# Attention steps and chunks of the gated projection moved in a written task list, values stored without zero blocks, and slopes that read PSUM

## The chip, the core and the metric

The kernel runs on one core of a Trainium2 chip. The metric is device time in microseconds (us), the median of three executions. A separate, profiled execution gives the trace that everything below is read from. The names of the engines are those of the profile: PE is the matrix engine, PEld its weight loads, DVE the vector engine, ACT the scalar engine, POOL the general engine and SP the engine that issues the DMAs.

## The reference

Three stages follow each other, all in float32:

```python
# 1. attention, q, k, v: (4 batches, 8 heads, 576, 64)
scores = q @ k.T / 8, masked: heads 0-3 see the last 32 positions,
         heads 4-7 every fourth of the last 128
x = softmax(scores) @ v                     # -> (2304, 512)
# 2. gated projection, d_ff = 1536
x = (sigmoid(x @ w_gate) * (x @ w_val)) @ w_out
# 3. second projection, d_ff = 2048
h = x @ w_in
g = maximum(h, 0) + alpha * minimum(h, 0)
out = g @ w_out2
```

## The kernel before

Every large product is made of three float16 matmuls ("passes": high by high, high by low, low by high half). So each weight and each activation is scaled and split into a high half (ACT) and a low half (DVE or POOL).

Attention is done per batch `b` in two half-batches, `hb = 2b` (plain window) and `hb = 2b + 1` (dilated). Its steps are `qk_mm` and `qk_sub` (scores and maximum), `exponent`, `p_sums`, `p_scale`, `transpose`, `p_hi`, `p_lo`, the splits of the values `v_hi` and `v_lo`, the products `pv_mm`, and `pv_x`, which splits the result into `xh[b]`. In `pv_mm` two heads of a pair share one matmul: 64 rows hold the keys of two heads, and the stationary value tile is 64 x 128, with one head's values in columns 0 to 63 and the other's in 64 to 127; the block of the wrong head is zero. To write these zeros, `v_hi` and `v_lo` run twice with the scale times 0 or 1 per row (`sides`, `v_scale`). A half-batch has 19 blocks x 3 passes x 2 pairs = 114 such matmuls; seven of the eight half-batches use them (the first uses float32, `pv32_mm`).

The gated projection of a batch has 12 chunks `m`: `gv_mm` for "g" and "v" (24 matmuls of 288 columns each), `gv_sigmoid` on ACT, `gv_multiply` on DVE, and `gv_halves`, the split into `gt[b, m]`. Then come four output columns `d` (`o1_mm`, 72 matmuls each, and `o1_y`, which stores the result). Three pairs of PSUM banks rotate among all g, v and o products.

What stands where is written out by hand. The head of the program, with attention of batches 0 and 1, all of batch 0's projection and the preparation of its weights, is the task list `FIRST`: a row such as `g 1 0 0` is a call, and each engine runs its instructions in the order of the calls. After it a loop goes over batches 1 to 3. In it, `attention(b + 1)` gives two tables, `before` and `after`, of steps keyed by chunk (0 to 11) or column (12 to 15), and `prepare` takes steps from a queue `steps` that decode, sum, split and store the weights of the second projection. Each call adds to a budget, and a step is taken when the budget covers its cost. The last batch ("late") also begins the second projection: `y_high`, `y_low` and `unit_short` between the columns of `o1_mm`.

The second projection is computed by a seven-product scheme on quarters. After the loop, 16 calls of `unit(j, k)` (four blocks `j` of tokens, four `k` each) make the hidden values; between their seven products, `spare()` puts the products of the output (`out2_mm`) of the block before. In a unit, `c1`, `c2` and `c4` are copied from PSUM by ACT (`copy`), `plus` adds such a copy to another product on DVE, `relu` makes the negative part on ACT, and `slopes` (two DVE instructions of 256 columns) adds it with its slope. The sums of quarters run on POOL (`g_sums`), and `high` and `g_low` split the hidden values.

## Time and profile before

| | us |
|---|---|
| median of 3 executions (886.60 to 889.74) | 888.07 |
| the profiled execution | 886.76 |
| its span, first to last instruction | 885.0 |
| PE busy | 831.8 (94%) |
| DVE busy | 660.7 (75%) |
| ACT busy | 450.8 (51%) |
| POOL busy | 300.4 (34%) |

A busy share is an average over stages with different limits: 94% of PE is made of long stretches in which it never waits, and of a few in which it does. What a change is worth is decided in the second kind. A row of the timeline gives, in brackets, how long the engine had been idle before it and what ended that. A granted clock of 1.00 is 2.4 GHz, one of 0.50 is 1.2 GHz; a figure between is a mean over the stretch.

### The profile page before, as it was taken

Reading aid. Unit: us, or ns where it says so; the run is one execution under the profiler, and the core shown is the slowest. Engines: PE = TensorE matmul, PEld = TensorE weight load, DVE = VectorE, ACT = ScalarE, POOL = GpSimd, SP = SyncE. Lnnn points to the kernel's source line nnn. Section 1 sums busy time; section 2 is a strip of 40 time slices with the busy share of each in tenths; the row PEclk is TensorE's granted clock in tenths of the full one; section 3 lists DMA queues with packets and bytes.
Section 4 is the critical chain, followed back from the end, with each engine's and each line's share of the span. In section 5 each row is a group of like instructions: output and inputs, shape, how many; then the busy total and the mean of one; then the engine's idle time right before and its main releaser. Section 6 shows DMA issues by size and latency. Waiting matters only on the chain.

```text
span 885.0 us, 19452 instructions
## 1 busy us (share of the span) xinstructions
PE 831.8 (94%) x8196; PEld 684.9 (77%) x8196; DVE 660.7 (75%) x1039; ACT 450.8 (51%) x739; POOL 300.4 (34%) x264
## 2 busy tenths in 40 slices
PE   7789687999999999999999989997999999999998
PEld 5467465777777777777788768886888888888887
...
GB/s 330 288 171 156 192 119 154 54 76 157 81 38 199 206 82 156 25 29 320 240 148 237 331 252 224 340 222 193 264 185 190 273 281 192 202 302 203 128 217 81
DMA packets 85175, 166.81 MB, mean 188 GB/s; under 512 B 5344, under 2 KB 57696, under 8 KB 85088
## 3 DMA queue, kind: packets, MB, share of 16 engines
...
HBM read 137.24 MB, written 28.31 MB: 187 GB/s over the span
## 4 chain that ended last, share of the span: by engine, by line
PE 52%; DVE 23%; ACT 10%; DMA 5%; issue 5%; POOL 3%; SPq 1%; ACTq 0%; DVEq 0%; POOLq 0%
PE banks L1206 14%; PE banks L963 13%; PE banks L589 12%; PE banks L631 10%; DVE plain L187 3%; DVE plain L183 3%; DVE temp_w L1009 2%; ACT junk L194 2%; DVE plain L179 2%; DMA plain_dram<-plain 2%; DVE gf L607 2%; DVE halves L823 2%; DVE temp_y L1009 2%; PE banks L323 1%; DMA w_dram<-halves 1%
## 5 line engine op out<-in xcount | busy, mean ns | idle before, releaser
L589 PE MATMUL banks<-xh,w_gv 128*128 128x288 f16 x2304 | 295.0, 289 | 7.5 <-DVE sc L156 3.3
L589 PEld LDWEIGHTS <-w_gv 128*128 128x128 f16 x2304 | 224.2, 99 | 67.9 <-issue 6.6
L963 PE MATMUL banks<-yh,w_i 128*128 128x256 f16 x1536 | 190.0, 275 | 13.1 <-ACT temp_y L1018 6.5
L963 PEld LDWEIGHTS <-w_i 128*128 128x128 f16 x1536 | 151.3, 99 | 33.6 <-issue 13.5
L631 PE MATMUL banks<-gt,w_o 128*128 128x288 f16 x1152 | 146.5, 288 | 3.6 <-DVE gf L607 1.8
L631 PEld LDWEIGHTS <-w_o 128*128 128x128 f16 x1152 | 112.2, 98 | 33.0 <-issue 3.0
L1206 PEld LDWEIGHTS <-g_gv 128*128 128x128 f16 x780 | 76.6, 98 | 9.1
L1206 PE MATMUL banks<-w,g_gv 128*128 128x256 f16 x612 | 75.5, 273 | 0.0
L1058 POOL TENSOR_TENSOR yh<-temp_y 128x512 f32<-128x512 f32 x16 | 27.0, 1690 | 131.6 <-DVE temp_y L1009 126.9
L164 POOL TENSOR_SCALAR sc<-sc 128x1 f32<-128x1 f32 x35 | 11.6, 333 | 167.8 <-DVE sc L160 167.7
L1009 DVE SCALAR_TENSOR_TENSOR temp_w<-neg,sc,temp_w 128x256 f32<-128x256 f32 x48 | 55.5, 1194 | 10.9 <-ACT neg L1001 10.8
L168 POOL TENSOR_TENSOR gt<-gf,gt 128x576 f16<-128x576 f32 x24 | 38.3, 1595 | 73.7 <-ACT gt L614 73.6
L1206 PEld LDWEIGHTS <-g_g 128*128 128x128 f16 x564 | 55.2, 98 | 6.4
L187 DVE SCALAR_TENSOR_TENSOR plain<-words,plain 128x512 uint32<-128x512 uint32 x68 | 56.9, 858 | 1.2
L194 ACT ACTIVATE junk<-plain 128x1024 bf16<-128x1024 f32 (+1 forms) x36 | 36.3, 1009 | 39.4 <-DVE plain L198 21.7
L602 ACT ACTIVATE sg<-banks,sc 128x576 f32<-128x576 f32 x48 | 35.3, 735 | 39.5 <-PE banks L589 28.5
L607 DVE SCALAR_TENSOR_TENSOR gf<-banks,sg 128x576 f32<-128x576 f32 x48 | 35.9, 749 | 25.1 <-PE banks L589 24.2
L183 DVE SCALAR_TENSOR_TENSOR plain<-words,plain 128x512 uint32<-128x512 uint32 x68 | 49.3, 746 | 1.2
L614 ACT ACTIVATE gt<-gf 128x576 f16<-128x576 f32 x48 | 32.4, 674 | 34.9 <-DVE gf L607 34.9
L1206 PE MATMUL banks<-w,g_g 128*128 128x256 f16 x396 | 48.3, 273 | 0.0
L179 DVE TENSOR_SCALAR plain<-words 128x512 uint32<-128x512 uint32 x68 | 34.6, 530 | 14.0 <-DMA plain_dram<-plain 6.2
L388 POOL TENSOR_TENSOR s<-s,rs 128x1152 f32<-128x1152 f32 (+1 forms) x9 | 17.3, 1925 | 72.0 <-DVE rs L383 65.5
...
## 6 DMA issues: line engine op xcount, KB each, us to landing
...
```

What stands on the lines that cost most here:

```text
L168: engine.tensor_tensor(out=lo, in0=src, in1=hi, op=ALU.subtract)
L179: nc.vector.tensor_scalar(out=d, in0=hi, scalar1=3, scalar2=0x3FFFFFFF, op0=ALU.logical_shift_left, op1=ALU.bitwise_and)
L183: nc.vector.scalar_tensor_tensor(out=d, in0=hi, scalar=0xC0000000, in1=d, op0=ALU.bitwise_and, op1=ALU.bitwise_or)
L187: nc.vector.scalar_tensor_tensor(out=d, in0=lo, scalar=29, in1=d, op0=ALU.logical_shift_right, op1=ALU.bitwise_or)
L194: nc.scalar.activation(junk[:, :src.shape[1]], src, AF.Square, accum_out=dst)
L589: nc.tensor.matmul(ps[:, h, :], lhsT=a, rhs=x_[:, H2 * h:H2 * h + H2], start=(kk == 0 and i == 0), stop=(kk == KD - 1 and i == 2),)
L602: nc.scalar.activation(halves(sg), ps, AF.Sigmoid, scale=sgx[b][:, m:m + 1])
L607: nc.vector.scalar_tensor_tensor(out=halves(gf), in0=ps, scalar=2.0 ** -15, in1=halves(sg), op0=ALU.mult, op1=ALU.mult)
L631: nc.tensor.matmul(ps[:, h, :], lhsT=a, rhs=x_[:, H2 * h:H2 * h + H2], start=(m == 0 and z == 0), stop=(m == M1 - 1 and z == 2),)
L963: nc.tensor.matmul(o, lhsT=h, rhs=l, start=(new and v == 0 and q == 1), stop=(q == total_), skip_group_check=True,)
L1009: nc.vector.scalar_tensor_tensor(out=temps[x_][:, c], in0=t[:, c], scalar=slope[:, u + v:u + v + 1], in1=src[:, c], op0=ALU.mult, op1=ALU.add,
L1206: nc.tensor.matmul(ps[:, H4 * t:H4 * t + H4].rearrange("p (c f) -> p c f", c=2), lhsT=a, rhs=x_, start=(first and k == 0 and t == 0 and z ...
```

## The change

It has four parts.

1. Values without zero blocks: `vh` holds the values once. `v_hi` and `v_lo` are one instruction each, and `v_scale` is gone. `pv_mm` takes 32 rows (one head) and a 64-column stationary tile, with the head choosing the upper or lower half of the output partitions: twice as many matmuls of the same width.
2. Slopes read PSUM: `plus` writes its sum back to PSUM (onto the bank of product 2, and onto that of product 7 for the last quarter), and `relu` and `slopes` read it there.
3. `FIRST` is written in another order, and takes in chunks 1 and 2 of batch 1 (before it held chunk 0 alone: three chunks now), the steps 0 to 6 of the attention of batch 2 (`hb` 4), and three calls of `prepare`. The loop for batch 1 starts at chunk 3 and skips those steps. Two `gt` tiles of batch 1 get places of their own.
4. In the loop, the `after` steps of a column come inside its loop over `m` (for `d == 2` at `m == 6`).

```diff
+    EARLY = 3
+    DONE = 7
-    NQ, NK, NV = 2 * NB * 64, 2 * (S + WINDOW), NB * P
+    NQ, NK, NV = 2 * NB * 64, 2 * (S + WINDOW), NB * 64
+    def v_hi(hb):
+        nc.scalar.activation(v_half(hb, 0), vc[hb], AF.Copy, scale=s_x[:, hb // 2:hb // 2 + 1])
+
+    def v_lo(hb):
+        nc.vector.scalar_tensor_tensor(
+            out=v_half(hb, 1), in0=vc[hb], scalar=s_x[:, hb // 2:hb // 2 + 1], in1=v_half(hb, 0), op0=ALU.mult,
+            op1=ALU.subtract,
         )
...
-            w = [v_[:, i, m].rearrange("p h d -> p (h d)") for i in range(2)]
-            for i, (a, x_) in enumerate(passes(w, p_)):
-                for pair, ps in enumerate(xt[hb, half]):
-                    k = slice(64 * pair, 64 * pair + 64)
...
+            for i, (a, x_) in enumerate(passes((v_[:, 0, m], v_[:, 1, m]), p_)):
+                for h in range(2):
+                    for pair, ps in enumerate(xt[hb, half]):
+                        k = slice(64 * pair + 32 * h, 64 * pair + 32 * h + 32)
+                        nc.tensor.matmul(
+                            ps[64 * h:64 * h + 64, WINDOW * (n0 - first):WINDOW * (n1 - first)], lhsT=a[k], rhs=x_[k],
...
-    def plus(x_, c, ps):
-        nc.vector.tensor_tensor(out=temps[x_], in0=ps, in1=temps[c], op=ALU.add)
+    def plus(dst, c, ps):
+        nc.vector.tensor_tensor(out=dst, in0=ps, in1=temps[c], op=ALU.add)
+        return dst
...
-        nc.vector.tensor_tensor(out=f11, in0=ps, in1=temps["c1"], op=ALU.add)
+        plus(ps_y, "c1", ps_y)
...
-        slopes(j, u, f"a11 {k % 2}", f11, t["a11"])
+        slopes(j, u, f"a11 {k % 2}", ps_y, t["a11"])
...
-        plus("a22", "c4", ps_z)
+        plus(ps_y, "c4", ps_z)
...
-        slopes(j, U + u, "a22", temps["a22"], t["a22"])
+        slopes(j, U + u, "a22", ps_y, t["a22"])
...
-        plus("a12", "c2", mm(4, "z"))
+        ps_z = plus(ps_z, "c2", mm(4, "z"))
...
-        def do(table, k):
-            if k in table:
+        def do(table, k, b):
+            if k in table and not (b == 1 and k < DONE):
...
-            for m in range(b == 1, M1):
+            for m in range(EARLY if b == 1 else 0, M1):
...
-2 0; oy 0 1; o 0 3 0; o 0 2 2; pvm 3 1; pvx 3 1 1; pvx 3 1 0; o 0 3 1; o 0 3 2; o 0 2 3; o 0 3 3; g 1 0 0; oy 0 2; v 1
+1 0; phi 4; g 1 1 1; half 1 0 0; plo 4; sig 1 1; v 1 1 0; prep 6; v 1 1 1; lv 6; mul 1 1; g 1 2 0; g 1 2 1; half 1 1;
```

What this does to the order on an engine is shown at three places. A row names a line of the program, the operation and its output and inputs; lines have other numbers in the two versions.

ACT at the end of `FIRST`. Before, from the third stored output column of batch 0 on (L649 stores a column, L602 is a sigmoid of a chunk of batch 1, L614 the high half of `gt`, L375 the exponent of `hb` 4):

```order
L649 ACTIVATE y<-banks,sc 128x576
L194 ACTIVATE junk,sc<-y 128x576
L649 ACTIVATE y<-banks,sc 128x576
L194 ACTIVATE junk,sc<-y 128x576
L602 ACTIVATE sg<-banks,sc 128x576
L614 ACTIVATE gt<-gf 128x576
L602 ACTIVATE sg<-banks,sc 128x576
L194 ACTIVATE junk,sc<-vc 128x1152
L614 ACTIVATE gt<-gf 128x576
L602 ACTIVATE sg<-banks,sc 128x576
L375 ACT_TABLE_LOAD
L375 ACTIVATE s<-s 128x1152
```

Of the change, from the third stored column on as well (L645, L595, L610 and L368 are the same four; L272 is `v_hi` of `hb` 4 and L403 its `p_hi`):

```order
L645 ACTIVATE y<-banks,sc 128x576
L195 ACTIVATE junk,sc<-y 128x576
L595 ACTIVATE sg<-banks,sc 128x576
L195 ACTIVATE junk,sc<-vc 128x1152
L368 ACT_TABLE_LOAD
L368 ACTIVATE s<-s 128x1152
L272 ACTIVATE vh<-vc,sc 128x1152
L645 ACTIVATE y<-banks,sc 128x576
L195 ACTIVATE junk,sc<-y 128x576
L403 ACTIVATE s<-pt 128x1152
L610 ACTIVATE gt<-gf 128x576
L595 ACT_TABLE_LOAD
```

The exponent, the value split and `p_hi` of `hb` 4 now stand ahead of the second sigmoid of batch 1, the first two of them ahead of the fourth output column of batch 0; before, the exponent came behind the third sigmoid.

ACT among the last chunks of the last batch. Before (L818 splits the output weights of the second projection; the first L602 of these rows is the sigmoid of chunk 9, the second that of chunk 10):

```order
L818 ACTIVATE halves<-quarter,sc 128x512 x3
L818 ACTIVATE halves<-plain,sc 128x512 x2
L818 ACTIVATE halves<-quarter,sc 128x512
L614 ACTIVATE gt<-gf 128x576
L602 ACTIVATE sg<-banks,sc 128x576
L818 ACTIVATE halves<-plain,sc 128x512
L818 ACTIVATE halves<-quarter,sc 128x512 x3
L818 ACTIVATE halves<-plain,sc 128x512
L614 ACTIVATE gt<-gf 128x576
L602 ACTIVATE sg<-banks,sc 128x576
L818 ACTIVATE halves<-plain,sc 128x512
```

Of the change (L814 is that split, L595 the sigmoid), the same first splits and what stands ahead of them:

```order
L595 ACTIVATE sg<-banks,sc 128x576
L195 ACTIVATE junk,sc<-plain 128x1024
L610 ACTIVATE gt<-gf 128x576
L595 ACTIVATE sg<-banks,sc 128x576
L610 ACTIVATE gt<-gf 128x576
L595 ACTIVATE sg<-banks,sc 128x576
L814 ACTIVATE halves<-quarter,sc 128x512 x3
L814 ACTIVATE halves<-plain,sc 128x512 x2
L814 ACTIVATE halves<-quarter,sc 128x512
L610 ACTIVATE gt<-gf 128x576
L595 ACTIVATE sg<-banks,sc 128x576
```

Before, 45 of the 48 sigmoids stand ahead of the first split and 14 splits come after the last sigmoid; in the change 43 stand ahead, and 7 come after. So the splits are two chunks earlier.

DVE in a unit of the first block of `unit`. Before (L1021 and L1130 are sums of `plus`, L1009 slopes, L1048 low halves, L1231 an output sum):

```order
L1021 TENSOR_TENSOR temp_w<-banks,temp_y 128x512
L1009 SCALAR_TENSOR_TENSOR temp_w<-neg,sc,temp_w 128x256 x2
L1130 TENSOR_TENSOR temp_w<-banks,yh 128x512
L1048 SCALAR_TENSOR_TENSOR g_g<-temp_w,sc,g_g 128x512
L1048 SCALAR_TENSOR_TENSOR g_g<-yh,sc,g_g 128x512
L1009 SCALAR_TENSOR_TENSOR temp_w<-neg,sc,temp_w 128x256 x2
L1231 SCALAR_TENSOR_TENSOR temp<-banks,sc,temp_y 128x256
```

Of the change:

```order
L1017 TENSOR_TENSOR banks<-banks,temp_y 128x512
L1005 SCALAR_TENSOR_TENSOR temp_w<-neg,sc,banks 128x256 x2
L1017 TENSOR_TENSOR banks<-banks,yh 128x512
L1045 SCALAR_TENSOR_TENSOR g_g<-temp_w,sc,g_g 128x512
L1045 SCALAR_TENSOR_TENSOR g_g<-yh,sc,g_g 128x512
L1005 SCALAR_TENSOR_TENSOR temp_w<-neg,sc,banks 128x256 x2
L1229 SCALAR_TENSOR_TENSOR temp<-banks,sc,temp_y 128x256
```

The order is the same; the sums are written to PSUM, and the slopes take them from there.

## Rows read from the trace of the kernel before

**Rows 1.** Windows by stage: us, then busy time of each engine, clock, DMA.

```profile
0.00:146.40 146.40, 115.30 (x1334) 84.70 (x1335) 124.43 (x224) 97.73 (x177) 75.84 (x77) 0.91 0.63 213
146.40:188.00 41.60, 39.47 (x411) 30.62 (x411) 21.91 (x35) 19.35 (x32) 15.96 (x17) 0.96 0.10 33
188.00:495.00 307.00, 304.90 (x3115) 242.47 (x3113) 230.71 (x365) 144.11 (x208) 56.79 (x46) 1.00 0.45 152
495.00:522.00 27.00, 21.74 (x166) 16.67 (x164) 16.91 (x20) 13.46 (x23) 17.71 (x15) 0.94 0.90 295
...
555.00:626.00 71.00, 62.33 (x558) 54.10 (x556) 53.95 (x88) 38.21 (x67) 28.09 (x26) 0.98 0.67 245
626.00:843.00 217.00, 216.94 (x1988) 194.29 (x1986) 174.72 (x252) 112.49 (x186) 86.32 (x64) 1.00 0.60 219
```

**Rows 2.** Timeline of PE, head: start, duration, instructions, idle before and its end.

```profile
106.24 0.16 PE L148 MATMUL banks<-sc,mask_sb 128*128 128x1 bf16 x1 [6.24 <-ACT junk L194]
...
146.42 6.02 PE L631 MATMUL banks<-gt,w_o 128*128 128x288 f16 x36 [1.83 <-DVE gf L607]
```

**Rows 3.** Low split of the values, by line: duration in ns, least, median, most; first and last start.

```profile
L282 DVE SCALAR_TENSOR_TENSOR vh<-vc,sc,vh x12: 1403/1409/3150, 92.8 to 379.5; 128x1152 f16<-128x1152 f32 x12
```

**Rows 4.** Groups by form: busy us, mean ns, then idle before.

```profile
L187 DVE SCALAR_TENSOR_TENSOR plain<-words,plain 128x512 uint32<-128x512 uint32 x68 | 56.9, 858 | 1.2
...
L183 DVE SCALAR_TENSOR_TENSOR plain<-words,plain 128x512 uint32<-128x512 uint32 x68 | 49.3, 746 | 1.2
...
L179 DVE TENSOR_SCALAR plain<-words 128x512 uint32<-128x512 uint32 x68 | 34.6, 530 | 14.0 <-DMA plain_dram<-plain 6.2 <-DMA words<-w_in 3.8 <-POOL w_gv L168 3.0
...
L172 DVE SCALAR_TENSOR_TENSOR w_gv<-plain,sc,w_gv 128x512 f16<-128x512 f32 x9 | 10.9, 1209 | 1.9 <-ACT w_gv L171 1.9
```

**Rows 5.** Timeline of PE around products of probabilities and values.

```profile
16.61 2.12 PE L452 MATMUL banks<-pt,vc 32*64 32x64 f32 x72 [1.57 <-DMA vc<-vk]
...
238.53 0.94 PE L437 MATMUL banks<-s,vh 64*128 64x64 f16 x54
239.40 0.79 PE L589 MATMUL banks<-xh,w_gv 128*128 128x288 f16 x5
```

**Rows 6.** Timeline, the step from the last weight splits to the second projection.

```profile
509.13 2.00 ACT L818 ACTIVATE halves<-quarter,sc 128x512 f16<-128x512 f32 x3 [4.08 <-DMA w_dram<-halves]
...
516.10 0.27 PE L963 MATMUL banks<-yh,w_i 128*128 128x256 f16 x1 [2.77 <-ACT yh L920]
```

**Rows 7.** Slopes and sums by line: duration in ns, least, median, most.

```profile
L1009 DVE SCALAR_TENSOR_TENSOR temp_w<-neg,sc,temp_w x48: 469/1400/1493, 563.9 to 846.9; 128x256 f32<-128x256 f32 x48
L1009 DVE SCALAR_TENSOR_TENSOR temp_y<-neg,sc,temp_y x48: 472/480/1491, 569.2 to 842.2; 128x256 f32<-128x256 f32 x48
L1009 DVE SCALAR_TENSOR_TENSOR temp_y<-neg,sc,banks x32: 472/476/481, 571.0 to 843.0; 128x256 f32<-128x256 f32 x32
...
L1021 DVE TENSOR_TENSOR temp_w<-banks,temp_y x16: 677/684/692, 572.6 to 844.1; 128x512 f32<-128x512 f32 x16
```

**Rows 8.** Timeline of PE, DVE and POOL, second to fourth unit.

```profile
588.09 1.47 PE L963 MATMUL banks<-yh,w_i 128*128 128x256 f16 x12
603.13 2.49 PE L963 MATMUL banks<-yh,w_i 128*128 128x256 f16 x12 [5.05 <-ACT temp_y L1018]
621.28 1.47 PE L963 MATMUL banks<-yh,w_i 128*128 128x256 f16 x12 [1.40 <-ACT temp_y L1018]
...
588.11 0.88 DVE L1009 SCALAR_TENSOR_TENSOR temp_y<-neg,sc,temp_y 128x256 f32<-128x256 f32 x2
592.99 2.80 DVE L1009 SCALAR_TENSOR_TENSOR temp_w<-neg,sc,temp_w 128x256 f32<-128x256 f32 x2 [0.76 <-ACT neg L1001]
595.71 0.68 DVE L1130 TENSOR_TENSOR temp_w<-banks,yh 128x512 f32<-128x512 f32 x1
599.57 1.88 DVE L1009 SCALAR_TENSOR_TENSOR temp_w<-neg,sc,temp_w 128x256 f32<-128x256 f32 x2
...
592.83 1.27 POOL L1059 TENSOR_TENSOR temp_y<-temp_y 128x512 f32<-128x512 f32 x1
```

More of the change, by code (lines that the diff above doesn't have):

```diff
@@ L235, in places @@
             ap.tile([P, 2, S + WINDOW], F32, tag="k", name="k"),
-            ap.tile([P, 2, NB, 2, 64], F16, tag="v", name="vh"),
+            ap.tile([P, 2, NB, 64], F16, tag="v", name="vh"),
         )
@@ L612, in gv_halves @@
         gf = open_.pop(("f", b, m))
-        t = gt[b, m] = gp.tile([P, 2, S], F16, tag="g", name="gt")
+        if b == 1 and m < EARLY - 1:
+            t = gt[b, m] = ap.tile([P, 2, S], F16, tag=f"g{m}", name="gt")
+        else:
+            t = gt[b, m] = gp.tile([P, 2, S], F16, tag="g", name="gt")
         nc.scalar.activation(t[:, 0, :], gf, AF.Copy)
@@ L1305, in attention_moe_kernel @@
         nc.sync.dma_start(out=mask_sb, in_=mask)
-        run(FIRST)
-        turn["first"] = False
         def attention(b):
@@ L1406, in prepare @@
                     w()
+        TASKS["prep"] = lambda n, sums=1: prepare(n, bool(sums))
+        run(FIRST)
+        turn["first"] = False
         def take(items):
@@ L1475, in attention_moe_kernel @@
                 gv_multiply(b, m)
-                do(before, m)
-                do(after, m)
+                do(before, m, b)
+                do(after, m, b)
                 prepare(3 - (0 if late else ATTENTION.get(m, 0)), sums=False)
@@ L1490, in attention_moe_kernel @@
                     x_gate_scale(b + 1, 0, M1)
-                do(before, M1 + d)
-                do(after, M1 + d)
+                do(before, M1 + d, b)
                 for m in range(M1):
+                    if m == (6 if d == 2 else 0):
+                        do(after, M1 + d, b)
                     if m in (2, 6, 10):
@@ L1588 @@
[L1588 to L1592 removed]
+lqk 0 3; warm 8 5; warm 6 2; lqk 1 3; qkm 0 0; lv 0; qks 0 0; qkm 0 1; lv 1; exp 0 0; qkm 0 2; qks 0 1 1; exp 0 1; qks
@@ new lines @@
+0 2 1; rs 0 0; exp 0 2; pm 0 0 0; rs 0 1; lgv 0; qkm 1 0 4; pm 0 1 0; qks 1 0; lqk 2; tr 0 0; tr 0 1; rs 0 2; exp 1 0;
+qkm 1 1 5; qks 1 1; lal; qkm 1 2 0; rs 1 0; pm 0 2 0; xb 0; tr 0 2; lgv 1; qks 1 2 1; exp 1 1; lgv 3; pm 1 0 0; xb 1;
+pv32 0 0 6; rs 1 1; pm 1 1 0; exp 1 2; lgv 2; dec 0 0; xsum 0 0; lv 3; xpow 0; rs 1 2; pm 1 2 0; tr 1 1; tr 1 0; phi 1
+1; pv32 0 1 4; dec 0 1; warm 14 3; plo 1 1; pvx 0 0 0; vhi 1; phi 1 0; tr 1 2; pvx 0 0 1; wb 0; lv 2; vlo 1; lgv 6;
+phi 1 2; plo 1 0 0; pvx 0 1 0; plo 1 2 0; wsum 0; pvx 0 1 1; pvm 1 0; wpow 0; dec 1; pvm 1 1 4; spl 0 0; pvx 1 0 0;
@@ new lines @@
+0 1; wpow 5; mul 0 2; exp 2; dec 6; sig 0 3; v 0 3 0; spl 5 0 1; v 0 3 1; xpow 1; mul 0 3; wb 6; g 0 4 0; spl 5 1 1;
+wsum 6; v 0 4 0; wgs 4; g 0 4 1; half 0 2 1; wpow 6; spl 6 0; wgs 5; v 0 4 1; g 0 5 0; lo 1 0; dec 7; sig 0 4; spl 6
+1; wb 7; half 0 3; wsum 7; g 0 5 1; rs 2; mul 0 4; wpow 7; wgs 7; g 0 6 0; dec 8; sig 0 5; spl 7 0; pm 2; spl 7 1; v 0
+5 0; lgv 9; wb 8; g 0 6 1; v 0 5 1; wsum 8; wgs 6; half 0 4; v 0 6 0; tr 2; lqk 3; lv 4; wpow 8; sig 0 6; mul 0 5; wgs
+8; phi 2; vhi 2; g 0 7 0; spl 8 0; v 0 6 1; g 0 7 1; dec 9; spl 8 1 1; wb 9; lo 0 2; sig 0 7; plo 2; wsum 9 0; mul 0
@@ new lines @@
+6; g 0 8 0; v 0 7 0; vlo 2; lgv 11; half 0 6 1; half 0 5 1; wpow 9; g 0 8 1; dec 10; pvm 2 0; pvx 2 0 1; spl 9 0; v 0
+7 1; spl 9 1 1; wb 10; wsum 10; mul 0 7; wpow 10; sig 0 8; dec 11; v 0 8 0; pvx 2 0 0; v 0 8 1; spl 10 0 1; wgs 9; spl
+10 1; wb 11; g 0 9 0; half 0 7 1; pvm 2 1; lo 0 1; lo 1 1; wsum 11; pvx 2 1 0; v 0 9 0; odec 0 0 1 2; wpow 11; orow 0
+1 1; lo 2 0; orow 0 0 0; pvx 2 1 1; v 0 9 1; g 0 9 1; qkm 3 0; lo 2 2; spl 11 0; mul 0 8; wgs 10; orow 0 2 0; qks 3 0;
+spl 11 1 1; qkm 3 1; g 0 10 0; vhi 3; obd 0 1; obd 0 0; odec 1 0 1; half 0 8 1; sig 0 9; osum 0; v 0 10 0; g 0 10 1;
@@ new lines @@
+mul 0 9; opow 0; lo 1 2; vlo 3; qkm 3 2; lo 3 1; v 0 10 1; v 0 11 0; odec 1 2; ospl 0 0 1; wgs 11; qks 3 2; orow 1 2
+0; xb 4; sig 0 10; lo 2 1; lo 3 2; qks 3 1; g 0 11 0; g 0 11 1; orow 1 0 1; mul 0 10; orow 1 1 0; ospl 0 1; odec 2 0 1
+2; obd 1 1; exp 3; obd 1 0; lqk 4; sig 0 11; v 0 11 1; half 0 9 0; osum 1; opow 1; orow 2 2 0; mul 0 11; o 0 0 0; obd
+2 1; half 0 11 1; lo 3 0; orow 2 0 1; orow 2 1 1; rs 3; half 0 10 1; ospl 1 0 1; o 0 0 1; obd 2 0; pm 3; osum 2; opow
+2; ospl 1 1; tr 3; o 0 0 2; odec 3 0 1 2; o 0 1 0; gs 1; phi 3; o 0 0 3; ospl 2 0 1; orow 3 2 0; plo 3 0 0; orow 3 1
@@ L1593 @@
+sig 1 2; prep 6; v 1 2 0; v 1 2 1; mul 1 2; prep 3
 """
```

75 lines of the change are left out of this document (18 added, 57 removed).

## The prediction

> **What bounds the kernel now.** I read the windows by stage first, to see where PE, the busiest engine, is not busy; then the timeline of PE in those stretches, for what ended each idle time; then the rows of the instructions that the change touches.
>
> The windows split the span in two kinds [rows 1]. From 188 to 495 us PE is busy 304.9 of 307.0 us, and from 626 to 843 us 216.94 of 217.0: there nothing can be won but by taking work from PE. It idles in three places: 146.4 - 115.3 = 31.1 us in the head, 27.0 - 21.7 = 5.3 us between 495 and 522 us, and 71.0 - 62.3 = 8.7 us between 555 and 626 us. The granted clock is below 1.00 in the same three, so part of what PE does there runs at 1.2 GHz.
>
> In the head DVE is busy 124.4 of 146.4 us [rows 1], and PE's long waits end with something that stood behind DVE: 6.24 us for a bound on ACT that reads decoded weights, and the first product with w_o at 146.42 us waits for the last gated values on DVE [rows 2]. Between 495 and 522 us the order is: the last weight splits on ACT wait 4.08 us for a DMA to free their place; `y_high` stands behind them on ACT; PE waits for it 2.77 us [rows 6], and for DVE's half of it in two more waits that are in the 5.3 us. Between 555 and 626 us PE waits 5.05 and 1.40 us for an ACT copy that frees a bank [rows 8], and that copy stands on ACT behind a high half that needs the slopes of DVE.
>
> **The change, part by part.** The sum is made against the profiled execution, 886.76 us (a span of 885.0 and 1.8 around it); the median shown is 888.07, 1.3 more, and I add that 1.3 at the end. A difference of 0.3% (2.7 us) is about what a measurement of this kernel can tell from none.
>
> *Slopes from PSUM.* 96 slopes instructions change their source. Those on temp_w take 1400 ns in the middle and 469 at best, those on temp_y 480 and 1491 at worst; the 32 that already read PSUM take 472 to 481, all of them [rows 7]. The long ones stand where POOL runs: at 592.99 us a pair takes 2.80 us while POOL has a sum at 592.83 us; at 588.11 us a pair takes 0.88 [rows 8]. So a slope with two sources in SBUF waits for POOL, and one with a source in PSUM does not. I take 0.88 for every pair. In a unit of this stretch that is 2.80 - 0.88 = 1.9 us ahead of the sum at 595.71 us, and 1.88 - 0.88 = 1.0 us for the pair at 599.57 us, both on the way to the copy that PE waits for at 603.13 us. The same 2.9 us are saved in the unit before, and DVE runs behind PE from one unit to the next, so 5.8 us stand against the wait of 5.05: it goes, and so does the one of 1.40. The 12 matmuls after the long wait take 2.49 us, where 12 take 1.47 before it [rows 8]: they ran at 1.2 GHz. The mean clock of 0.98 over these 71 us [rows 1] is 2.8 us at that level, which cost PE half of them, 1.4 us; with no long wait ahead I expect these back. Against that I leave 1 us for what becomes late next, the weights' DMA, which leads PE by little once PE does not wait. Term: -5.05 - 1.4 - 1.4 + 1 = about -7 us. What has no row is `plus` with its output in PSUM: the same sum into SBUF takes 684 ns for 512 columns, a PSUM slope 476 for 256 [rows 7]. Per column these are 1.3 and 1.9 ns, so between 0.68 and 0.95 us, or +0.3 us at most for each of three sums in a unit, and as little below; I take no change, the nearest row being the sum itself. In the long stretch from 626 us PE is never idle, so the other units give nothing.
>
> *Steps of the second projection's weights.* The three `prep` calls come in place of those of two loop passes, and the loop's own calls go on, so the queue runs ahead: the splits L818 stand two chunks earlier against the sigmoids. A chunk is 48 matmuls, at 304.9 / 3115 = 0.098 us each in the long stretch [rows 1]: two chunks are over 9 us, more than the waits of 4.08 and 2.77 us [rows 6]. What is late next is `o1_mm`, whose PE work is dense. Of the 5.3 us idle I take 4, and 1 us for the clock (0.94 over 27 us is 3.2 us at 1.2 GHz, 1.6 lost): -5 us. Bounds: 0, if the chain of DMAs, and not its place in the order, sets the end; -7, if all goes.
>
> *The head.* Up to the first product with w_o the new list has three low splits of values fewer on DVE (half-batches 1 to 3, 1.41 us each [rows 3]), 4.2 us. The product waits for the multiply of chunk 10 [rows 2], and ahead of that one stand three decodes fewer (now behind it), each 0.53 + 0.75 + 0.86 = 2.14 us [rows 4], 6.4 us; but two more weight splits on DVE at 1.21 [rows 4], 2.4 us, and one row scaling and one low half, which I put at a step of the decode each, 1.6. Sum: -4.2 - 6.4 + 2.4 + 1.6 = -6.6 us for the start of that product. Chunks 1 and 2 of batch 1 and the steps of `hb` 4 are moved, not added: up to the end of chunk 2 every engine has the same work as before but for the value splits, and from 146 to 188 us DVE is busy only 21.9 of 41.6 us [rows 1], which covers the moved steps. I take -6. Bounds: -12, more than half of the 22 us in which DVE idles in the head; and 0, where w_o's later columns, whose decodes now come behind the multiplies, are late instead. The moved loads (`lqk 5`, `lv 6`) find the DMA engines 10% busy in that stretch [rows 1].
>
> *Values without zeros.* Each of seven half-batches has 57 passes of two matmuls on two row groups; now they are four, on four row groups. 54 matmuls took 0.87 us [rows 5], so a pass of two takes 32 ns, and the two run side by side. If four do so as well, nothing is added. The nearest row with 32-row, 64-column tiles is the float32 product, 72 instructions in 2.12 us, 59 ns for two [rows 5]; if a pass takes that long, it is 27 ns x 57 x 7 = 10.8 us more on PE. I take 6 ns more, close to the lower end, since that row streams float32: 0.34 us for each half-batch, and five of them lie where PE is never idle: +1.7 us. What the splits save on DVE and ACT after the head is hidden behind PE.
>
> On this the Trainium skill speaks against the change: "TensorEngine Tiling (Array Packing)", "Gotcha 2: Feature Incompatibilities", has it that column tiling shuts out the fast weight load, and the new stationary tile of 64 columns is column tiled. By the page "TensorE: Matmul & The Clock Gate", section "LDWEIGHTS (loading the stationary operand)", 64 columns then load in 64 / 1.2 = 53 ns, an estimate; were a pass bound by that, 21 ns would be added to each, 8.4 us in all. No row before shows such a load in float16. It is one of the rivals below, priced there by a row.
>
> *The steps in the column loop* move by less than a column; PE idles 2.1 us in all of that stretch, and I take 0.
>
> Sum: -7 - 5 - 6 + 1.7 = -16.3, so 870.5, and with the 1.3 of the median 871.8: 872.
>
> **The rivals.**
>
> *The head gives nothing.* For it: 31 us of idle time in many small pieces, and every list has its own. Against it: DVE's work ahead of the product is less by 6.6 us. Time: 878.
>
> *The weights' chain is bound by its DMAs, and the two chunks of lead are lost.* This is also the case that the change does not do what the order says. For it: the wait before the splits is for a DMA [rows 6], and DMA is 90% busy there [rows 1]. Time: 877.
>
> *Loads bound the pass of four*, so that it takes as long as the two of the float32 row, 59 ns [rows 5]: 27 ns x 57 x 5 = 7.7 us on the half-batches where PE is never idle, in place of 1.7. Against it: float32 streams longer. Time: 878. The fast weight load's loss, in the Trainium skill's page on tiling above, would be its cause.
>
> *More goes in the head*, 12 us or more, with the clock at 1.00 and the other terms at their ends: 861.
>
> *Slower: four tiles do not run side by side.* Each of 57 x 7 = 399 passes is then four single matmuls. A single one is not below 32 / 2 = 16 ns, its share now, and not above 32; at 32, 128 - 32 = 96 ns are added, 38 us in all. With the other terms at -18 that is 888.07 + 20 = 908. It decides from 18 us / 399 = 45 ns a pass on: with passes of 77 ns or more the kernel is slower than before. Against it: two row groups run side by side now.
> Beside it stands a rule of the Trainium skill: "TensorE: Matmul & The Clock Gate", section "Wait — 56ns, not 53.3ns?", has matmuls start no closer than 25 ns apart, which would make a pass 100 ns. The trace does not agree for the two row groups: 54 of them in 0.87 us are 16 ns apart [rows 5].
>
> *The bank is held longer.* The bank of product 2 is now free only when the slopes of the second quarter are done. In the third unit the next product 2 starts at 588.09 us, and those slopes end at 588.99 [rows 8]: PE would wait 0.9 us there. For it: DVE runs behind PE. Against it: DVE is ahead by 2.9 us a unit now. If that gain stays away, no -7 and 15 waits of up to 0.9 us, 13.5: 888.07 - 5 - 6 + 1.7 + 13.5 = 892.
>
> **How the numbers follow.** Forecast 872: 0.44. Head nothing, 878: 0.14. Chain bound, 877: 0.09. Loads, 878: 0.08. More, 861: 0.13. Tiles one by one, 908: 0.06. Bank held, 892: 0.06. The forecast's own range, with its terms' bounds half used, is 864 to 881. The range for 8 in 10 goes from 861 to 886: it takes in the first five cases and leaves out the two slow ones and the tails. Faster by over 0.3% (below 885.4): the first five, 0.88, less 0.08 for several terms failing together, 0.80; within it 0.09; slower 0.11.
>
> **What would show it.** PE's first product with w_o starts at 140 us or before, where it stood at 146. No PE wait over 1 us for an ACT copy in the units of the first block, and slopes at 0.48 us each whatever POOL does. The splits of the output weights end before PE asks for `y_high`. A block of 54 products with the values became 108 in under 1.2 us. The forecast is wrong if the end of chunk 2 of batch 1 is not earlier (head), if a block of 108 takes over 2 us (tiles), or if PE waits for DVE before product 2 (bank).

## The result and the profile after

The kernel after took 871.94 us in the median (871.76 to 872.18, 4 runs), the kernel before 887.81 beside it (886.6 to 889.74): a ratio of 0.9819, 95% interval 0.9801 to 0.9838. The forecast was 872.0. The profiled execution took 872.18 us, with a span of 870.4 and a mean granted clock of 0.99.

The total came out as forecast; its terms did not. To see it, I cut both traces at the same products on PE: the start of the first product with w_o (the output weights of the gated projection), the end of chunk 2 of batch 1, the end of batch 3's gated chunks, the end of the short units, the end of the fourth 512-token unit, the end of the last unit. The stretch from batch 3's chunks to the end of the short units is called the jam here, for the waits of 495 to 522 us that it held before. The length of each stretch in us, each from one profiled execution (the forecast's -6 for the head stands as -6.6 to the first product and +0.6 behind it):

| stretch | forecast | before | after | difference |
|---|---|---|---|---|
| to the first product with w_o | -6.6 | 146.4 | 137.5 | -8.9 |
| to the end of chunk 2, batch 1 | +0.6 | 61.3 | 68.7 | +7.4 |
| middle, to the end of batch 3's chunks | +1.7 | 286.2 | 285.1 | -1.1 |
| jam, to the end of the short units | -5 | 59.9 | 52.7 | -7.2 |
| units 1 to 4 | -7 | 70.9 | 66.3 | -4.6 |
| units 5 to 16 | 0 | 218.3 | 218.1 | -0.2 |
| to the end of the span | 0 | 41.9 | 42.0 | 0 |

Windows of the kernel after, by these stages (us, busy time of each engine, clock, DMA share, GB/s):

```profile
0.00:137.50 137.50, 110.26 (x1562) 83.02 (x1563) 119.99 (x217) 91.41 (x171) 65.19 (x71) 0.96 0.67 223
137.50:190.70 53.20, 48.84 (x651) 38.01 (x650) 34.08 (x58) 25.24 (x39) 19.52 (x19) 0.97 0.21 74
190.70:206.30 15.60, 13.64 (x98) 10.35 (x98) 11.21 (x14) 7.62 (x11) 4.98 (x4) 0.89 0.58 192
206.30:491.30 285.00, 283.79 (x3341) 226.41 (x3340) 214.94 (x335) 131.26 (x194) 57.09 (x47) 1.00 0.46 157
491.30:512.00 20.70, 20.70 (x173) 16.70 (x171) 12.77 (x13) 9.65 (x17) 14.39 (x14) 1.00 0.84 283
544.00:612.00 68.00, 62.37 (x572) 54.41 (x571) 49.10 (x92) 39.78 (x70) 28.56 (x27) 1.00 0.72 262
```

Against [rows 1]: the jam is gone (PE busy all of 20.7 us, clock 1.00 for 0.94), and the units idle 5.6 us for 8.7, at full clock. But behind the first product with w_o, where PE idled 2.1 us of 41.6 before, it now idles 53.20 - 48.84 + 15.60 - 13.64 = 6.3 us, at a clock down to 0.89.

The timeline of PE there has the three waits that make these 6.3 us:

```profile
137.51 4.57 PE L627 MATMUL banks<-gt,w_o 128*128 128x288 f16 x36
144.74 0.19 PE L149 MATMUL banks<-sc,mask_sb 128*128 128x1 bf16 x2 [2.66 <-ACT junk L195]
...
167.57 0.95 PE L430 MATMUL banks<-s,vh 32*64 32x64 f16 x95 [1.66 <-issue]
...
192.66 14.57 PE L582 MATMUL banks<-xh,w_gv 128*128 128x288 f16 x104 [1.99 <-ACT y L645]
```

The first is the sum of w_o's third chunk (`osum 2`), which waits for ACT to add up the squares of that chunk; the second is inside the product of probabilities and values (PV) and waits for no semaphore ("issue"); the third is the product `g 1 1 0`, which needs the bank that ACT's eviction of `oy 0 3` frees. On ACT that eviction itself waited 2.34 us for a scale that POOL computes behind the attention's scaling:

```profile
188.20 2.12 POOL L381 TENSOR_TENSOR s<-s,rs 128x1152 f32<-128x1152 f32 x1 [23.32 <-DVE sc L157]
190.29 1.31 POOL L165 TENSOR_SCALAR sc<-sc 128x1 f32<-128x1 f32 x1
191.58 0.26 POOL L635 TENSOR_SCALAR sc<-sc 128x1 f32<-128x1 f32 x1
191.87 0.74 ACT L645 ACTIVATE y<-banks,sc 128x576 f32<-128x576 f32 x1 [2.34 <-POOL sc L635]
```

In the timeline of PE, the product of probabilities and values in the dense stretch answers to [rows 5] (54 matmuls took 0.87 us):

```profile
235.63 1.06 PE L430 MATMUL banks<-s,vh 32*64 32x64 f16 x108
236.62 3.12 PE L582 MATMUL banks<-xh,w_gv 128*128 128x288 f16 x24
```

From one start to the next row's, 108 matmuls took 0.99 us. The slopes and sums by line (ns: least, median, most) answer to [rows 7]:

```profile
L1005 DVE SCALAR_TENSOR_TENSOR temp_y<-neg,sc,banks x80: 473/476/481, 559.3 to 827.7; 128x256 f32<-128x256 f32 x80
L1005 DVE SCALAR_TENSOR_TENSOR temp_w<-neg,sc,banks x64: 467/476/483, 513.1 to 830.8; 128x256 f32<-128x256 f32 x64
...
L1017 DVE TENSOR_TENSOR banks<-banks,temp_y x32: 686/693/700, 557.2 to 828.8; 128x512 f32<-128x512 f32 x32
```

No slope takes over 483 ns, where 1400 was the middle of 48 before; a sum into PSUM costs 9 ns more than one into SBUF. In the stretch of [rows 8] the timeline of PE now has, beside the wait of 1.09 us ahead of its first unit, which stood there in the kernel before as well, five short ones:

```profile
588.91 1.47 PE L959 MATMUL banks<-yh,w_i 128*128 128x256 f16 x12 [1.03 <-ACT temp_y L1014]
...
591.68 1.47 PE L959 MATMUL banks<-yh,w_i 128*128 128x256 f16 x12 [0.64 <-DVE banks L1017]
...
594.55 1.49 PE L959 MATMUL banks<-yh,w_i 128*128 128x256 f16 x12 [0.75 <-DVE temp_y L1005]
...
603.34 0.83 PE L959 MATMUL banks<-yh,w_i 128*128 128x256 f16 x6 [0.75 <-DMA w_i<-wi_dram]
605.54 0.83 PE L959 MATMUL banks<-yh,w_i 128*128 128x256 f16 x6 [1.38 <-DMA w_i<-wi_dram]
```

What still takes both its sources from SBUF is the low halves. Ahead of the wait of 0.64 us one of them takes 1.75 us on DVE, where 0.75 is the middle of its group, beside a sum on POOL:

```profile
588.21 1.75 DVE L1045 SCALAR_TENSOR_TENSOR g_y<-temp_w,sc,g_y 128x512 f16<-128x512 f32 x1
...
587.68 1.73 POOL L1059 TENSOR_TENSOR temp_w<-temp_w,yh 128x512 f32<-128x512 f32 x1
```

DVE is not idle from there to the sum at 590.94 us that PE waits for, so these 1.0 us more stand against that wait; no run here moves them.

### The profile page after: what moved, and what is told of

Read it like the earlier page. It is cut to its first block, busy times and chain, and to the rows that moved or that the text cites. A ratio compares the mean times of both kernels' runs of the same rounds, so it can differ in the third digit from the quotient of the medians.

```text
span 870.4 us, 21028 instructions
## 1 busy us (share of the span) xinstructions
PE 826.0 (95%) x8994; PEld 684.1 (79%) x8994; DVE 619.6 (71%) x1031; ACT 441.3 (51%) x730; POOL 287.3 (33%) x261
## 4 chain that ended last, share of the span: by engine, by line
PE 75%; DVE 12%; ACT 4%; DMA 2%; issue 2%; POOL 1%; SPq 0%; ACTq 0%; DVEq 0%; POOLq 0%
PE banks L582 25%; PE banks L1204 18%; PE banks L959 17%; PE banks L627 12%; DVE plain L188 2%; DVE plain L184 2%; DMA words<-w_val 1%; DVE plain L180 1%; PE banks L316 1%; PE banks L430 1%; DMA w_i<-wi_dram 1%; DVE w_gv L173 1%; DVE g_g L1045 1%; DVE plain L199 1%; ACT junk L195 1%
## 5 line engine op out<-in xcount | busy, mean ns | idle before, releaser
L959 PE MATMUL banks<-yh,w_i 128*128 128x256 f16 x1536 | 187.2, 273 | 5.6 <-DMA w_i<-wi_dram 2.1
L997 ACT ACTIVATE neg<-banks 128x512 f32<-128x512 f32 x72 | 42.8, 594 | 56.6 <-DVE banks L1017 40.5
L169 POOL TENSOR_TENSOR gt<-gf,gt 128x576 f16<-128x576 f32 x24 | 35.1, 1466 | 64.4 <-ACT gt L610 64.4
L595 ACT ACTIVATE sg<-banks,sc 128x576 f32<-128x576 f32 x48 | 35.3, 735 | 40.1 <-PE banks L582 32.9
L188 DVE SCALAR_TENSOR_TENSOR plain<-words,plain 128x512 uint32<-128x512 uint32 x68 | 52.9, 799 | 1.2
L610 ACT ACTIVATE gt<-gf 128x576 f16<-128x576 f32 x48 | 32.2, 675 | 42.2 <-DVE gf L600 42.2
L184 DVE SCALAR_TENSOR_TENSOR plain<-words,plain 128x512 uint32<-128x512 uint32 x68 | 49.8, 754 | 1.2
L1045 DVE SCALAR_TENSOR_TENSOR g_gv<-temp_w,sc,g_gv 128x256 f16<-128x256 f32 (+1 forms) x37 | 26.0, 711 | 28.0 <-ACT g_gv L1041 28.0
L1005 DVE SCALAR_TENSOR_TENSOR temp_w<-neg,sc,banks 128x256 f32<-128x256 f32 x64 | 27.8, 476 | 25.1 <-ACT neg L997 25.1
```

The costliest lines, as they stand in the source:

```text
L169: engine.tensor_tensor(out=lo, in0=src, in1=hi, op=ALU.subtract)
L184: nc.vector.scalar_tensor_tensor(out=d, in0=hi, scalar=0xC0000000, in1=d, op0=ALU.bitwise_and, op1=ALU.bitwise_or)
L188: nc.vector.scalar_tensor_tensor(out=d, in0=lo, scalar=29, in1=d, op0=ALU.logical_shift_right, op1=ALU.bitwise_or)
L595: nc.scalar.activation(halves(sg), ps, AF.Sigmoid, scale=sgx[b][:, m:m + 1])
L959: nc.tensor.matmul(o, lhsT=h, rhs=l, start=(new and v == 0 and q == 1), stop=(q == total_), skip_group_check=True,)
L997: nc.scalar.activation(t[:, :2 * n], src[:, :2 * n], AF.Relu, scale=-1.0)
```

## The experiments

All times are medians of device us, ratios are to the kernel before, timed beside it on the same chip (886.98 to 887.53 in the median). The same cuts as above, one profiled execution of each kernel:

| kernel | to 1st w_o | to chunk 2 | middle | jam | units 1-4 | units 5-16 |
|---|---|---|---|---|---|---|
| before | 146.4 | 61.3 | 286.2 | 59.9 | 70.9 | 218.3 |
| after | 137.5 | 68.7 | 285.1 | 52.7 | 66.3 | 218.1 |
| after, again | 137.1 | 68.0 | 285.3 | 52.6 | 65.9 | 218.1 |
| values only | 144.4 | 61.6 | 285.3 | 60.3 | 70.9 | 219.8 |
| first list back | 145.5 | 61.4 | 286.7 | 59.3 | 65.9 | 218.1 |
| slopes back | 135.5 | 68.3 | 285.1 | 52.6 | 70.9 | 219.5 |
| fewer steps | 134.1 | 68.6 | 285.7 | 59.6 | 65.8 | 218.1 |
| lead on before | 146.4 | 60.9 | 293.5 | 52.6 | 70.9 | 218.3 |
| PV early | 138.4 | 66.6 | 287.4 | 52.8 | 65.9 | 218.1 |
| osum | 137.0 | 68.5 | 285.1 | 52.6 | 65.6 | 218.1 |
| scales | 136.7 | 67.4 | 285.1 | 52.6 | 65.6 | 218.1 |
| both | 137.4 | 64.2 | 285.1 | 52.8 | 66.3 | 218.1 |
| both, o 0 2 0 later | 137.1 | 63.4 | 285.4 | 52.8 | 66.0 | 218.1 |
| and qkm 3 2 earlier | 135.3 | 64.5 | 285.1 | 52.6 | 65.9 | 218.1 |

Read down a column, a stretch moves mainly where the edit touches it. The first two columns also move by themselves: nine executions with one and the same order up to the first product with w_o span 134.1 to 138.4 us there, and the four of them with the same order to the end of chunk 2 (after, after again, slopes back, PV early) take 66.6 to 68.7 us for the second stretch. In the last column, "values only" and "slopes back" hold one wait for the w_i DMA each (1.51 and 1.03 us) that the others do not have; I did not look for its cause.

**Values without zeros, alone, on the kernel before.**

```
-            for h in range(2): ... nc.scalar.activation(w[:, 0, :, h, :], t, AF.Copy, scale=v_scale[:, c:c + 1])
+        nc.scalar.activation(v_half(hb, 0), vc[hb], AF.Copy, scale=s_x[:, hb // 2:hb // 2 + 1])
...
+                        k = slice(64 * pair + 32 * h, 64 * pair + 32 * h + 32)
```

> The kernel before with the values without zeros alone (one ACT and one DVE instruction for a half-batch's values, 32-row tiles in PV); the old opening list, the old slopes. By the theory (PV dearer by 0.26 us a half-batch from hb 1 on, seven of them, and the head's freed ACT and DVE time worth nothing by itself): 887 to 890 against 887.8, PV blocks of 108 in 0.99 us. Rival one (the shorter chain of values in the head lets the gate weights and w_o start earlier): 884 or less, first product with w_o before 145. Rival two (the doubled PV instructions starve TensorE): 890 or more, with stalls inside PV blocks that end with the issue and not with a semaphore.

885.89 us, 0.9982 (0.9971 to 0.9993): 1.6 us faster (0.6 to 2.6), better than the theory, worse than rival one. PV does cost more, 0.99 us for 108 as in the kernel after, but the idle time of PE in the middle falls from 2.1 to 0.5 us, as the window of that stretch shows:

```profile
206.00:491.30 285.30, 284.80 (x3369) 227.22 (x3369) 213.72 (x342) 131.52 (x192) 55.81 (x45) 1.00 0.46 158
```

and the head is 2.0 us shorter up to the first product with w_o in this one profile (0.9 us in that of the next run). In the middle at least, what the splits no longer do on ACT and DVE was not all hidden.

**The old list on the kernel after.**

```
-    EARLY = 3
-    DONE = 7
+    EARLY = 1
+    DONE = 0
...
-FIRST = (the new list)
+FIRST = (the list of before, with one vhi and one vlo for each half-batch)
```

> The kernel after with the old opening list and the old split of work behind it (no chunk 0 to 2 of batch 1, no attention steps, no preparation steps in the list); values without zeros and slopes from PSUM kept. By the theory the new list and its lead are worth 7.3 in the jam at 495 to 522, some 1.4 in the head and 1 in the middle: 880 to 883. Rival one (the jam was closed by the slopes or the values, the list is worth the head alone): 873 to 875. Rival two (most of the whole gain is the list's): 885 or more.

880.72 us, 0.9927 (0.9914 to 0.994). The jam is back, 59.3 us, the two stretches of the head trade as before, and the middle is 1.6 us longer: the theory. Against the kernel after the list is worth 0.0108 in the ratio, 9.6 us; against the values alone, the slopes, with the edit of the column loop that this kernel keeps, are worth 0.0055, 4.9 us.

**The slopes from SBUF again, in the kernel after.**

```
-        plus(ps_y, "c1", ps_y)
+        plus(temps[f"a11 {k % 2}"], "c1", ps_y)
...
-        slopes(j, U + u, "a22", ps_y, t["a22"])
+        slopes(j, U + u, "a22", temps["a22"], t["a22"])
```

> The kernel after with the sums and slopes of a 512-token unit read from SBUF as before; list and values kept. By the theory the two waits of 5.05 and 1.40 us in the first block's units come back, less the clock that they cost: 876 to 879, with a slope instruction of 1.4 us or more beside the gated halves on POOL ahead of each wait. Rival one (those waits hung on the lateness of the jam, not on the source of the slopes): 872 to 873.5. Rival two (the slopes cost in every block): 885 or more.

875.49 us, 0.9865 (0.9852 to 0.9878), 4.1 us over the kernel after by the ratios, and just under the theory's 876. Units 1 to 4 take 70.9 us again, though the jam ahead of them is as short as after. Rival one is out. The timelines of DVE, POOL and PE show the wait and its cause:

```profile
580.57 2.81 DVE L1005 SCALAR_TENSOR_TENSOR temp_w<-neg,sc,temp_w 128x256 f32<-128x256 f32 x2 [0.76 <-ACT neg L997]
...
580.42 1.27 POOL L1056 TENSOR_TENSOR temp_y<-temp_y 128x512 f32<-128x512 f32 x1
581.64 1.46 POOL L1057 TENSOR_TENSOR yh<-yh,temp_y 128x512 f32<-128x512 f32 x1
...
590.72 2.50 PE L959 MATMUL banks<-yh,w_i 128*128 128x256 f16 x11 [5.06 <-ACT temp_y L1014]
```

The same pair in the kernel after takes 0.87 us, beside the first of the same two sums on POOL, and ends before the second starts:

```profile
581.70 0.87 DVE L1005 SCALAR_TENSOR_TENSOR temp_w<-neg,sc,banks 128x256 f32<-128x256 f32 x2 [0.72 <-ACT neg L997]
...
581.57 1.27 POOL L1056 TENSOR_TENSOR temp_y<-temp_y 128x512 f32<-128x512 f32 x1
582.81 1.26 POOL L1057 TENSOR_TENSOR yh<-yh,temp_y 128x512 f32<-128x512 f32 x1
```

**Fewer preparation steps in the list, in the kernel after.**

```
-... v 1 1 0; prep 6; v 1 1 1; ... sig 1 2; prep 6; v 1 2 0; v 1 2 1; mul 1 2; prep 3
+... v 1 1 0; prep 3; v 1 1 1; ... sig 1 2; prep 3; v 1 2 0; v 1 2 1; mul 1 2
```

> The kernel after with 6 columns of the second projection's preparation in the opening list in place of 15, as many as the kernel before had given by the end of chunk 2. All else is kept. By the theory the lead of the steps is what closes the jam: 7 comes back, 878 to 880, with TensorE waiting for the output-weight split between 490 and 525 again. Rival one (the jam was closed by the freed ACT and DVE time or by the clock, not by the lead): 872 to 873. Rival two (half the lead is enough, the rest is slack): 874 to 876.

878.32 us, 0.9892 (0.9877 to 0.9906), 6.5 us over the kernel after by the ratios. The jam is back to 59.6 us and nothing behind the head has moved by more than 0.6 us; the head of its profiled execution (875.63 us) is the shortest of all. The stretch to the end of chunk 2 is as long as in the kernel after, 68.6 us, so the nine columns more of preparation are not what makes it long. ACT's splits wait for the same DMA and PE for `y_high` behind them, as in [rows 6]:

```profile
502.64 2.03 ACT L814 ACTIVATE halves<-quarter,sc 128x512 f16<-128x512 f32 x3 [3.06 <-DMA w_dram<-halves]
...
510.09 0.27 PE L959 MATMUL banks<-yh,w_i 128*128 128x256 f16 x1 [2.23 <-ACT yh L916]
```

**The same lead on the kernel before, alone.**

```
-... v 1 0 1; oy 0 3; sig 1 0; mul 1 0
+... v 1 0 1; oy 0 3; sig 1 0; mul 1 0; prep 6; prep 6; prep 3
```

> The kernel before, with three preparation steps of the second projection (15 columns) put at the end of its old opening list and nothing else changed. By the theory the lead of these steps alone closes the jam at 495 to 522: 880 to 881.5 against 887. Rival one (the steps cost in the head, behind chunk 0 of batch 1, what they give in the jam, since DVE and the DMA queues do them there in place of other work): 885 to 888. Rival two (the lead helps only with the rest of the new list): 884 to 887, with the wait for the output-weight split still between 490 and 520.

886.3 us, 0.9992 (0.9982 to 1.0003): no gain, and my theory of a free lead falls. The jam is closed as in the kernel after, 52.6 us, 7.3 less. But the middle is 293.5 us, 7.3 more: rival one's exchange, only that the price is paid in the middle and not in the head. PE idles 8.6 us there for 2.1, and the longest of its waits, in its timeline, are

```profile
286.83 0.36 PE L437 MATMUL banks<-s,vh 64*128 64x64 f16 x13 [1.48 <-POOL s L168]
...
407.24 0.91 PE L437 MATMUL banks<-s,vh 64*128 64x64 f16 x52 [2.17 <-POOL s L168]
...
434.67 1.02 PE L589 MATMUL banks<-xh,w_gv 128*128 128x288 f16 x7 [1.84 <-ACT y L649]
```

Before the second of them, on DVE, the decodes that now come two chunks earlier stand ahead of the transposition that POOL's low part waits for:

```profile
399.70 0.69 DVE L183 SCALAR_TENSOR_TENSOR plain<-words,plain 128x512 uint32<-128x512 uint32 x1
400.43 0.69 DVE L187 SCALAR_TENSOR_TENSOR plain<-words,plain 128x512 uint32<-128x512 uint32 x1
401.22 0.69 DVE L198 TENSOR_TENSOR plain<-plain,sc 128x512 f32<-128x512 f32 x1
401.83 1.37 DVE L406 STREAM_TRANSPOSE pt<-s 128x1152 f32<-128x1152 f32 x1
...
395.22 2.12 POOL L388 TENSOR_TENSOR s<-s,rs 128x1152 f32<-128x1152 f32 x1 [24.19 <-DVE rs L383]
404.48 2.71 POOL L168 TENSOR_TENSOR s<-pt,s 128x1152 f16<-128x1152 f32 x1 [7.14 <-ACT s L410]
```

Its input was there at 397.34 us, 4.5 us before it starts. In the kernel before it starts as soon as that input is there:

```profile
396.04 1.38 DVE L406 STREAM_TRANSPOSE pt<-s 128x1152 f32<-128x1152 f32 x1 [2.01 <-POOL s L388]
```

So the lead is free only with something else of the change; the first two of the waits are in front of PV in column group 2, the very place that the change's edit of the column loop touches.

**That edit undone, in the kernel after.**

```
-                    if m == (6 if d == 2 else 0):
+                    if m == 0:
                         do(after, M1 + d, b)
```

> The kernel after with the one edit of the column loop undone: PV of the second half-batch's first half is issued ahead of the six products of column group 2 again, not behind them. By the theory (the steps' lead puts decodes of the second projection into the stretches where the attention's low parts on POOL are made, and this edit gives them six products more) TensorE waits for POOL's low parts before PV near 280 and 400 again, 1.5 and 2.2 us as in the kernel before with the lead alone: 874 to 876. Rival (the shorter chain of values without zeros or the attention done early covers the lead, and the edit is worth nothing, as the forecast had it): 870 to 872.

872.76 us, 0.9841 (0.9825 to 0.9857), between the two expected ranges. The waits come back where they were expected, somewhat shorter:

```profile
282.40 1.02 PE L430 MATMUL banks<-s,vh 32*64 32x64 f16 x104 [1.39 <-POOL s L169]
...
401.10 1.02 PE L430 MATMUL banks<-s,vh 32*64 32x64 f16 x104 [1.68 <-POOL s L169]
```

The middle takes 287.4 us for 285.1 and 285.3, so the edit is worth 2.1 to 2.3 us there. The median, 0.8 to 1.9 us over the kernel after's two (2.0 to 2.6 by the ratios), does not separate it by itself: the intervals overlap. Of the 7.3 us that the lead costs in the kernel before, the edit covers some 2; the rest is covered by other parts of the change. I take the shorter value splits and the attention that is done in the head for them; they were not taken apart.

**The two waits behind the first product with w_o.** The kernel after ran again beside three variants of its list.

> The kernel after, unchanged, beside the three variants of its opening list, so that differences of 1 or 2 us are read on one chip. 871.5 to 872.5 by every theory.

870.87 us, 0.9812 (0.9791 to 0.9832); its ratio and the first one's, 0.9819, agree within their intervals.

```
-... pm 3; osum 2; opow 2; ospl 1 1; tr 3; o 0 0 2; odec 3 0 1 2; ...
+... pm 3; ospl 1 1; tr 3; o 0 0 2; osum 2; opow 2; odec 3 0 1 2; ...
```

> The kernel after with the sum of w_o's third chunk (osum 2 and opow 2) moved in the list behind the next product, o 0 0 2. By the theory (from 137.5 us on TensorE's own work is the bound, so a wait there costs what it lasts) the wait of 2.66 us at 144.7 is filled with a product of 2.4 us: 869 to 870, and up to 1.7 more where the clock does not fall behind it. Rival (the third chunk's halves are late by as much, and the wait moves to the product that reads them): 871.5 to 872.5, with a new wait before o 0 2 0.

870.6 us, 0.9818 (0.9794 to 0.9841): no gain, the rival. The wait of 2.66 us has become one of 2.64 before the product that reads the third chunk, for its low half on DVE, in PE's timeline:

```profile
144.18 0.19 PE L149 MATMUL banks<-sc,mask_sb 128*128 128x1 bf16 x2 [0.45 <-ACT junk L195]
...
154.65 7.97 PE L627 MATMUL banks<-gt,w_o 128*128 128x288 f16 x50 [2.64 <-DVE w_o L173]
```

The second variant computes the scales of column groups 1 to 3 at once, ahead of POOL's other work:

```
-        if b == 0:
-            y_scale(b, d, d + 1)
+        if b == 0 and d < 2:
+            y_scale(b, d, KD if d else 1)
```

> The kernel after with the output scales of the first batch's last three column groups computed in one POOL instruction, ahead of the attention's scaling on POOL, in place of one instruction each. By the theory ACT's eviction of the fourth group then starts when TensorE ends it, not 1.2 us later behind POOL, and g 1 1 0 gets its bank 1.2 earlier: 870 to 871, to 869 if the clock holds. Rival (the bank comes free no earlier, since ACT has other work there, or the next wait takes it over): 871.5 to 872.5.

869.19 us, 0.9797 (0.9774 to 0.982). In PE's timeline the wait falls from 1.99 to 0.83 us:

```profile
192.16 2.12 PE L582 MATMUL banks<-xh,w_gv 128*128 128x288 f16 x16 [0.83 <-ACT y L645]
```

in size as expected; 1.7 us in the median is too little to be told from none. The third has both edits and PE's next product ahead of that wait:

```
-... v 1 0 1; mul 1 0; o 0 3 2; vhi 4; vlo 4; o 0 3 3; oy 0 3; tr 4; g 1 1 0; ...
+... o 0 3 2; vhi 4; vlo 4; o 0 3 3; oy 0 3; v 1 0 1; mul 1 0; tr 4; g 1 1 0; ...
```

> Both edits, and v 1 0 1 and its product put behind oy 0 3, so that TensorE has 1.6 us of work while ACT evicts the fourth column group. By the theory both waits (2.66 and 1.99 us) are gone: 866.5 to 868.5. Rival (the head is paced by the decoded weights or by DVE, and TensorE waits elsewhere for as long): 871 to 872.5.

865.33 us, 0.976 (0.9738 to 0.9783): 5.5 us under the kernel after beside it, the intervals apart. More than expected, since one wait is still there (154.94 us, 2.64 for w_o's low half, as in the first variant). Gone are the wait for ACT's eviction and the stall inside PV, and the clock is higher. The window from the first product with w_o to chunk 2's end:

```profile
137.40:201.60 64.20, 60.97 (x750) 47.40 (x748) 42.93 (x69) 30.71 (x47) 22.59 (x19) 0.97 0.31 107
```

The same window of the kernel after's second run:

```profile
137.10:205.10 68.00, 62.45 (x749) 48.33 (x748) 45.31 (x71) 32.84 (x50) 24.50 (x22) 0.95 0.30 102
```

PE idles 3.2 us there in place of 5.5; with a clock of 0.97 for 0.95 (0.03 x 64.2 and 0.05 x 68.0 us, 1.5 apart) that is the 3.8 us of the table. The profiled execution of this variant took 867.63 us, 3.1 under that of the kernel after; two of the other four took 864.0 and 863.7, at a mean clock of 0.994, and no trace shows where they gained more.

Two more tried to fill what is left:

```
-... o 0 2 0; o 0 1 2; ...
+... o 0 1 2; o 0 2 0; ...
```

> The kernel with both edits of the opening list's end, and o 0 2 0 put behind o 0 1 2, so that the third chunk's halves have 2.4 us more. By the theory the wait of 2.64 us before o 0 2 0 falls to 0.3 and the clock does not fall behind it: 861 to 863.5. Rival (the halves of the third and fourth chunk follow each other on DVE and ACT, and o 0 2 1 or o 0 3 0 waits in its place): 864.5 to 866.

866.54 us, 0.9772 (0.9749 to 0.9795): the rival, but at the sum of the fourth chunk (`osum 3`), which stands in the list ahead of the products that it named. In PE's timeline the wait before `o 0 2 0` falls to 0.44 us and that sum waits in its place:

```profile
155.05 4.09 PE L627 MATMUL banks<-gt,w_o 128*128 128x288 f16 x32 [0.44 <-DVE w_o L173]
...
162.89 0.19 PE L149 MATMUL banks<-sc,mask_sb 128*128 128x1 bf16 x2 [2.76 <-ACT junk L195]
```

The other, with `qkm 3 2` also put ahead of `osum 0`:

> The kernel before this one, with the scores qkm 3 2 put ahead of the sum of w_o's first chunk, where TensorE waited 2.83 us for ACT. By the theory (TensorE has work without a break from there on) its 0.9 us fills a part of that wait: 860 to 862.5, 0.9 less than the other. Rival (its bank or its q and k are not free by then and the sum is late): as the other or up to 2 more.

865.84 us, 0.9765 (0.9742 to 0.9789). The wait ahead of that sum is 1.07 us shorter (1.76 for 2.83), but the one ahead of the third chunk's sum is 1.17 longer (1.87 for 0.70), and the time is the same within what can be told. 865 to 866 us is the best that I found, 2.4% under the kernel before.

## Why the forecast was right in the sum and not in its terms

*Head: mechanism right, its end wrong.* The first product with w_o came 8.9 us earlier (6.6 forecast), but the end of chunk 2 only 1.4 (1.4 to 4.0 in the four profiles with the same order up to there), and the term was -6. The step that failed is the sentence that between 146 and 188 us the idle time of DVE covers the moved steps. Its first half, that every engine has the same work up to the end of chunk 2, was wrong as well: DVE is busy 165 us up to there where it was 156, in part because the list gives 15 columns of preparation where 6 were given. But with 6 again DVE is busy 160 us and the stretch is as long, so DVE's total was not the matter: single instructions on POOL and ACT were late for PE. The 7.4 us that the stretch is longer are 4.2 of waits (6.3 for 2.1), about 1.7 of clock (0.03 x 53.2 + 0.11 x 15.6 us, for 0.04 x 41.6 before), one score product of 0.9 that now lies ahead of its end, and 0.3 of PV. I had named this as a rival ("the head gives nothing"), for another reason, at 0.14. That two of the waits could be taken out again is shown by the variant with both edits, 3.8 us in this stretch and 5.5 in the median.

*Values: wrong sign.* The pass grew by 4.4 ns (0.99 - 0.87 us over 27 passes), 6 forecast; what failed is "what the splits save on DVE and ACT after the head is hidden behind PE". PE's 2.1 us of waits in the middle hung on just these engines, and 1.6 of them went. Alone the edit gives 1.6 us where I had +1.7 and head gains counted elsewhere.
The load-bound rival is out: 4.4 ns a pass, not 27. The rule on column tiling of the Trainium skill ("TensorEngine Tiling (Array Packing)", "Gotcha 2: Feature Incompatibilities") would have added 21 ns by the estimate in the prediction; no time of that size shows here. The 25 ns between matmuls of the Trainium skill's page "TensorE: Matmul & The Clock Gate", section "Wait — 56ns, not 53.3ns?", do not hold for four tiles either: 108 in 0.99 us are 9 ns apart.

*Steps: right in the place, and paid for by an edit that I had put at 0.* -7.2 for -5: all of the 5.3 us of idle time and the clock went, the term's own lower bound of -7. The lead alone does it (59.6 and 52.6 us with fewer steps and with the lead on the kernel before). But on the kernel before it takes 7.3 us in the middle. So the sentence that the steps in the column loop "move by less than a column", taken as 0, is the step that failed here: I had looked at PE's idle time of before, 2.1 us, and not at what the earlier steps would stand in front of. The edit is worth 2 us with the lead.

*Slopes: mechanism right, size off.* -4.6 (5.0 against the mean of the kernels with PSUM slopes) for -7. Both named waits went, and the 1.4 us of clock. The mis-sized term is the "1 us for what becomes late next": it is 3.4 us. In it are the w_i DMA (0.75 and 1.38, where 1.00 stood before), the copy on ACT (1.03, just over what I had allowed), a sum (0.64, behind the slow low half), and once, 0.75 us, the bank held by the second quarter's slopes, which is the rival "the bank is held longer" in small. Net, idle time fell by 3.0 us.
The row behind it, no slope over 483 ns beside POOL's sums, agrees with the Trainium skill, "SBUF — State Buffer", section "Who interferes with whom": a DVE instruction with two SBUF inputs contends with a POOL instruction that reads SBUF, one with at most one SBUF input, outside the two-port modes, does not.

So four errors in this pair of profiles, +4.6, -2.8, -2.2 and +2.4 us, cancel to within 2. The 1.3 us that I added because the median before lay that far above its profiled execution hide most of the rest: by the profiled executions it is 872.18 us for 870.5. That 872 was met so closely is luck, and no proof of its parts.
